# The second product of an MLP by seven half-size products instead of eight, tokens in chunks of 256

## The chip, the core and the metric

The kernel runs on one core of a Trainium2 chip. The core has a tensor engine (PE, with its weight loads shown apart as PEld), VectorE (DVE), ScalarE (ACT), GpSimd (POOL) and a queue that issues transfers (SP). The metric is the device time of one execution in microseconds, as the median of several runs. A profile shows one execution, instruction by instruction.

## The reference

Clustered attention makes `x` of shape (4, 768, 512): four batches, eight heads, each query attends to the keys of its own cluster. What follows is a token mix of rank 32 and an MLP with a residual:

```python
h = xt @ U @ V                      # xt = x with tokens last
u = x + h.transpose(0, 2, 1)        # (4, 768, 512)
ch = np.maximum(u @ w_ch1, 0.0) @ w_ch2   # 512 -> 2048 -> 512
return (u + ch).astype(np.float32)
```

The weights reach the kernel as the bits of float64 numbers, and the kernel turns them into float32 itself.

## The kernel before

**Order of work.** Everything is written as a plan: `at(time, fn, *args)` enters a call with a due time in plan units, the list is sorted by time, and the calls are issued in that order. `keep_order` ties the instructions of each engine to that order, so an engine never overtakes its own queue. Attention takes 16 head pairs of 12 units; the MLP begins at `M0`, in plan units, and there one unit was one inner tile of one chunk. The last of attention and of the mix (`values`, `sums`, `normalise`, `mix_u`, `mix_sum`, `mix_v`) is due after M0 and is interleaved with the first units of the MLP.

**Split products.** A float32 matrix is held as a high part, rounded to the type fp32r, and a low part, the remainder. A product is the sum of three: high x high, high x low, low x high. So each logical matmul is three instructions, each with a weight load of 128 columns.

**The MLP.** The 3072 tokens were eight chunks of 384 (`nh = 2 * B`), the 2048 inner features 16 tiles `f` of 128. For each chunk `turn_u` transposes the rows `u` (L595) and writes the parts `uh` and `ul` (ACT L597, DVE L598). `gemm1(i, f)` is 4 x 3 matmuls of 384 columns into a PSUM tile `ps_h` (L606 to L608); then ACT writes `hh`, the high part of relu (L611), and DVE `hl`, the low part (L612). `gemm2(i, f)` comes 1.2 units later: for each of three token tiles three matmuls of 512 columns (L622 to L624), accumulated over all 16 tiles in a bank `y`. `finish(i)` adds `y` to `u` on DVE (L630) and sends it out (L631).

**The weights.** Four groups `g` of four inner tiles. `load_weights(g, step, stage)` takes one raw tile [128, 512] through six stages with the due times in `stages`: a DMA into `rw` (L151), `upper` on ACT (L159) into `rw_g`, three bit operations on DVE, `join` (L171 to L174 in one go for groups 0 and 1; L178, L180, L183 for groups 2 and 3) into `rw_t`, and last the split: the high part on ACT (L204), the low part on POOL, or for a few tiles of group 1 on DVE (L205). Group 0 is made early in attention, group 1 in its last five head pairs' time, groups 2 and 3 while the MLP runs. Group 1 and 2 lie in `arena`, the space of attention's operands.

**Near M0.** `weights` (L492) adds up the attention weights `T`, mostly on POOL, for some steps of the last pair on DVE. All PSUM tiles of attention, transposes and `gemm1` are turned round in one pool of four, `ps_w`; `y` has four banks of its own.

Of the kernel before, what the change touches and what calls it, by code (L numbers as in the profile page):

```python
# [117 lines left out]
def clustered_attention_moe(ctx: ExitStack, tc: tile.TileContext, qk, v, cen, moe_U, moe_V, w1, w2, out):  # L118
# [8 lines left out]
    raw = ctx.enter_context(tc.tile_pool(name="raw", bufs=2))  # L127
    rows = ctx.enter_context(tc.tile_pool(name="rows", bufs=2, side="right"))
    ps_w = ctx.enter_context(tc.tile_pool(name="ps_w", bufs=4, space=PSUM, side="right"))

# [23 lines left out]
    def upper(rw):  # L154

        r, n = rw.shape
        g = raw.tile([P, 512], F32, name="rw_g")[0:r, 0:n]
        high = rw.bitcast(I32).rearrange("p (n two) -> p n two", two=2)[:, :, 1].bitcast(F32)
        nc.scalar.mul(g, high, 2.0 ** -112)  # L159
        return rw, g.bitcast(I32), None  # L160

    def join(rw, g, t, k):
# [4 lines left out]
        if k is None:  # L167

            b = work("ps_t").bitcast(I32)[0:r, 0:n]
            t = raw.tile([P, 512], I32, name="rw_t")[0:r, 0:n]  # L170
            nc.vector.tensor_scalar(b, g, 3, None, op0=ALU.logical_shift_left)  # L171
            nc.vector.scalar_tensor_tensor(out=b, in0=g, scalar=-0x80000000, in1=b,
                                           op0=ALU.bitwise_and, op1=ALU.bitwise_or)
            nc.vector.scalar_tensor_tensor(out=t, in0=low, scalar=29, in1=b,  # L174
                                           op0=ALU.logical_shift_right, op1=ALU.bitwise_or)
        elif k == 0:
            t = raw.tile([P, 512], I32, name="rw_t")[0:r, 0:n]
            nc.vector.tensor_scalar(t, g, 3, None, op0=ALU.logical_shift_left)  # L178
        elif k == 1:
            nc.vector.scalar_tensor_tensor(out=t, in0=g, scalar=-0x80000000, in1=t,  # L180
                                           op0=ALU.bitwise_and, op1=ALU.bitwise_or)
        else:
            nc.vector.scalar_tensor_tensor(out=t, in0=low, scalar=29, in1=t,  # L183
                                           op0=ALU.logical_shift_right, op1=ALU.bitwise_or)
        return rw, g, t

    parts, pool = {}, {}

    def load_weights(g, step, stage):
# [4 lines left out]
        elif stage == 1:  # L194
            parts[g, step] = upper(parts[g, step])
        elif stage < 5:
            if g > 1:
                parts[g, step] = join(*parts[g, step], stage - 2)
            elif stage == 3:
                parts[g, step] = join(*parts[g, step], None)  # L200
        else:
            w = parts.pop((g, step))[2].bitcast(F32)
            hi, lo = wg[g][2 * k][:, i, :], wg[g][2 * k + 1][:, i, :]
            nc.scalar.copy(hi, w)  # L204
            (nc.vector if g == 1 and step in (1, 2, 3, 5) else nc.gpsimd).tensor_sub(lo, w, hi)  # L205


    def weight_tile(g, name, pool):
        return pool.tile([P, 4, 512], F32R, name=f"{name}{g}", bufs=1)

    names = ("w1h", "w1l", "w2h", "w2l")
# [11 lines left out]

    wg[1] = [in_arena(2 * XS + 2048 * k, 4, 512) for k in range(4)]
    wg[2] = [in_arena(2048 * k, 4, 512) for k in range(3)]

# [36 lines left out]

    c_sb = raw.tile([P, 512], F32, name="rw_g").rearrange("p (n d) -> p n d", n=NP)
    c_rn = one.tile([P, NP], F32, name="c_rn")
    c_sq = raw.tile([P, 512], F32, name="rw_g")[:, 0:NP * D].rearrange("p (n d) -> p n d", n=NP)
    c_n = [one.tile([P, NP], F32, name=f"c_n{k}") for k in range(3)]
# [37 lines left out]
    def load_mix(k, stage):  # L305
# [17 lines left out]

# [24 lines left out]
    def largest(i):  # L348
# [218 lines left out]

    nh = 2 * B

    free = 2 * XS + 4 * 2048  # L570
    turned = {0: [in_arena(free, ND, HS), in_arena(free + ND * HS, ND, HS)]}

    def open_mlp():
# [3 lines left out]
        pool["y"] = ctx.enter_context(tc.tile_pool(name="ps_y", bufs=4, space=PSUM, reuse_waits="tile"))  # L577
        wg[2].append(weight_tile(2, "w2l", sb))
        turned[1] = [sb.tile([P, ND, HS], F32R, name=name) for name in ("uh", "ul")]

    def open_weights():
        tail.close()
        right = ctx.enter_context(tc.tile_pool(name="wpool3", bufs=1, side="right", reuse_waits="tile"))
        wg[3] = [weight_tile(3, name, right) for name in names]

    def fetch_u(i):
        b, h = divmod(i, 2)
        live["u", i] = rows.tile([P, HT, DM], F32, name="u", tag="R")
        nc.sync.dma_start(out=live["u", i], in_=u_scr[b][:, h * HT:(h + 1) * HT, :])

    def turn_u(i, d):

        ps = work("ps_uT")
        for t in range(HT):
            nc.tensor.transpose(ps[:, t * P:(t + 1) * P], live["u", i][:, t, d * P:(d + 1) * P], ident)  # L595
        hi, lo = (x[:, d, :] for x in turned[i % 2])
        nc.scalar.copy(hi, ps[:, 0:HS])  # L597
        nc.vector.tensor_sub(lo, ps[:, 0:HS], hi)  # L598

    def gemm1(i, f):  # L600
        w1h, w1l, _, _ = wg[f // FG]
        uh, ul = turned[i % 2]
        fs = slice((f % FG) * P, (f % FG) * P + P)
        ps = work("ps_h")
        for d in range(ND):
            nc.tensor.matmul(ps[:, 0:HS], w1h[:, d, fs], uh[:, d, :], start=(d == 0), stop=False)  # L606
            nc.tensor.matmul(ps[:, 0:HS], w1h[:, d, fs], ul[:, d, :], start=False, stop=False)  # L607
            nc.tensor.matmul(ps[:, 0:HS], w1l[:, d, fs], uh[:, d, :], start=False, stop=(d == ND - 1))  # L608
        hh = pool["sb"].tile([P, HS], F32R, name="hh", bufs=3)
        hl = pool["sb"].tile([P, HS], F32R, name="hl", bufs=3)  # L610
        nc.scalar.activation(hh, ps[:, 0:HS], AF.Relu)  # L611
        nc.vector.scalar_tensor_tensor(out=hl, in0=ps[:, 0:HS], scalar=0.0, in1=hh, op0=ALU.max, op1=ALU.subtract)  # L612
        live["h", i, f] = hh, hl

    def gemm2(i, f):
        if f == 0:
            live["y", i] = [pool["y"].tile([P, 512], F32, name=f"y_{t}", tag="y") for t in range(HT)]
        y, (hh, hl) = live["y", i], live.pop(("h", i, f))
        _, _, w2h, w2l = wg[f // FG]
        for t in range(HT):  # L620
            ts = slice(t * P, (t + 1) * P)
            nc.tensor.matmul(y[t], hh[:, ts], w2h[:, f % FG, :], start=(f == 0), stop=False)  # L622
            nc.tensor.matmul(y[t], hh[:, ts], w2l[:, f % FG, :], start=False, stop=False)  # L623
            nc.tensor.matmul(y[t], hl[:, ts], w2h[:, f % FG, :], start=False, stop=(f == NF - 1))  # L624

    def finish(i):
        b, h = divmod(i, 2)
        u, y = live.pop(("u", i)), live.pop(("y", i))
        for t in range(HT):
            nc.vector.tensor_add(u[:, t, :], y[t], u[:, t, :])  # L630
            nc.sync.dma_start(out=out[b, (h * HT + t) * P:(h * HT + t + 1) * P, :], in_=u[:, t, :])  # L631

# [83 lines left out]
    for g, pace in enumerate((NS, 2.04, 1, 1)):  # L716
        for stage, step in enumerate(stages[f"g{g}"]):
# [4 lines left out]
    at(M0 + 8.05, open_weights)  # L722
    for i in range(nh):
        m = M0 + NF * i
        at(m + (-10.98 if i else -15.06), fetch_u, i)
        for d in range(ND):
            at(m + (-4.5 + d if i else -1.52), turn_u, i, d)
        for f in range(NF):
            at(m + f, gemm1, i, f)
            at(m + f + 1.2, gemm2, i, f)  # L730
        at(m + 16.35, finish, i)

# [32 lines left out]
```

## Time and profile before

| | us |
|---|---|
| median of 3 runs | 1021.26 (1020.79 to 1023.74) |
| span of the profiled execution, first to last instruction | 1018.5 |
| PE busy | 990.5 |
| PEld busy | 786.9 |
| DVE busy | 490.5 |
| ACT busy | 347.7 |
| POOL busy | 359.4 |
| first `gemm1` matmul starts at | 463.13 |
| last matmul starts at | 1014.21 |

The median of the runs lies 2.8 us above the span. Busy time of PE is not PE at its peak: matmuls are pipelined and their shown durations overlap, so the distance from one start to the next tells what a matmul costs in a stream. A line such as `L606` is the line of the kernel above; `y<-w2l,hh` reads as output and inputs; `x288` is a count. In a list of groups the last columns are busy time, mean ns of one, the idle time of that engine before them and what ended it.

### The profile page before, as it was taken

Reading aid. Unit: us, or ns where it says so; the run is one execution under the profiler, and the core shown is the slowest. Engines: PE = TensorE matmul, PEld = TensorE weight load, DVE = VectorE, ACT = ScalarE, POOL = GpSimd, SP = SyncE. Lnnn points to the kernel's source line nnn. Section 1 sums busy time; section 2 is a strip of 40 time slices with the busy share of each in tenths; the row PEclk is TensorE's granted clock in tenths of the full one; section 3 lists DMA queues with packets and bytes.
Section 4 is the critical chain, followed back from the end, with each engine's and each line's share of the span. In section 5 each row is a group of like instructions: output and inputs, shape, how many; then the busy total and the mean of one; then the engine's idle time right before and its main releaser. Section 6 shows DMA issues by size and latency. Waiting matters only on the chain.

```text
span 1018.5 us, 13723 instructions
## 1 busy us (share of the span) xinstructions
PE 990.5 (97%) x5368; PEld 786.9 (77%) x5368; DVE 490.5 (48%) x914; ACT 347.7 (34%) x572; POOL 359.4 (35%) x246
## 2 busy tenths in 40 slices
PE   5899999999999999989999999999999999999998
PEld 3566666676667666657899999999999999998997
DVE  5797777777777666768772121121221211212211
ACT  4454554555556554564341111111111111111110
POOL 5466676888788967753230000000000000000000
PEclk9899999999999999999999999999999999999999
DMA  7754554656465636243431001010010010100000
GB/s 186 191 130 115 157 146 122 192 155 156 100 199 136 150 86 181 61 143 108 163 123 63 1 32 32 1 62 1 1 63 1 18 46 1 62 1 1 32 1 32
DMA packets 28687, 87.71 MB, mean 86 GB/s; under 512 B 4880, under 2 KB 9488, under 8 KB 28112
## 3 DMA queue, kind: packets, MB, share of 16 engines
q1 hardware_dynamic: 28240, 86.76, 30.5%
q8 instruction: 42, 0.69, 0.3%
q14 instruction: 21, 0.17, 0.1%
q10 hardware_dynamic: 384, 0.10, 0.0%
HBM read 42.99 MB, written 12.58 MB: 55 GB/s over the span
## 4 chain that ended last, share of the span: by engine, by line
PE 90%; DVE 5%; ACT 1%; issue 1%; POOL 1%; DMA 1%; ACTq 0%; SPq 0%; POOLq 0%; DVEq 0%
PE o_ps L500 12%; PE ps_h L606 9%; PE ps_h L608 9%; PE ps_h L607 9%; PE y L624 9%; PE y L623 9%; PE y L622 9%; PE ps_max L453 7%; PE st L477 6%; PE st L479 6%; DVE m L455 2%; PE ps_sum L512 1%; PE ps_sim L343 1%; PE ps_oT L533 1%; PE ps_uT L595 1%
## 5 line engine op out<-in xcount | busy, mean ns | idle before, releaser
L492 POOL TENSOR_TENSOR T<-T,pr 128x768 f32<-128x768 f32 x120 | 226.5, 1887 | 44.9 <-ACT pr L482 19.3
L612 DVE SCALAR_TENSOR_TENSOR hl<-ps_h,hh 128x384 fp32r<-128x384 f32 x128 | 71.2, 556 | 349.9 <-ACT hh L611 349.8
L455 DVE TENSOR_REDUCE m<-ps_max 128x1 f32<-128x384 f32 x384 | 195.2, 547 | 80.6 <-PE ps_max L453 79.0
L611 ACT ACTIVATE hh<-ps_h 128x384 fp32r<-128x384 f32 x128 | 62.9, 491 | 373.8 <-PE ps_h L608 373.8
L482 ACT ACTIVATE pr<-st 128x768 f32<-128x768 f32 x192 | 154.3, 812 | 83.5 <-PE st L479 65.4
L453 PE MATMUL ps_max<-arena 128*128 128x384 f32 x384 | 126.6, 380 | 6.9 <-DVE oh L369 2.5
L500 PE MATMUL o_ps<-pr,vt 128*64 128x384 f32 x768 | 132.2, 494 | 0.1
L623 PE MATMUL y<-w2l,hh 128*128 128x512 f32 x288 | 113.6, 395 | 0.0
L477 PE MATMUL st<-arena 128*128 128x384 f32 x384 | 104.9, 354 | 2.0 <-ACT pr L482 2.0
L453 PEld LDWEIGHTS ps_max<-arena 128*128 128x128 f32 x384 | 70.5, 192 | 45.4 <-issue 21.4
L500 PEld LDWEIGHTS o_ps<-pr,vt 128*64 128x64 f32 x768 | 52.7, 138 | 66.4 <-issue 59.8
L479 PE MATMUL st<-arena 97*128 97x384 f32 x384 | 99.2, 340 | 2.8 <-DMA arena<-mT 2.8
L477 PEld LDWEIGHTS st<-arena 128*128 128x128 f32 x384 | 66.2, 190 | 17.9 <-issue 9.3
L492 POOL TENSOR_TENSOR T<-pr 128x768 f32<-128x768 f32 x30 | 56.6, 1886 | 62.2 <-ACT pr L482 62.2
L624 PE MATMUL y<-w2h,hl 128*128 128x512 f32 x192 | 76.1, 396 | 0.0
L624 PE MATMUL y<-arena,hl 128*128 128x512 f32 x192 | 76.0, 396 | 0.0
L622 PE MATMUL y<-w2h,hh 128*128 128x512 f32 x192 | 75.1, 391 | 0.0
L622 PE MATMUL y<-arena,hh 128*128 128x512 f32 x192 | 74.8, 390 | 0.0
L479 PEld LDWEIGHTS st<-arena 97*128 97x128 f32 x384 | 70.4, 190 | 3.5 <-issue 2.2
L623 PEld LDWEIGHTS y<-w2l,hh 128*128 128x128 f32 x288 | 54.0, 188 | 9.1
L504 ACT COPY os<-o_ps 128x384 f32<-128x384 f32 x32 | 15.3, 480 | 104.7 <-PE o_ps L500 104.7
L606 PE MATMUL ps_h<-arena,w1h 128*128 128x384 f32 x128 | 44.8, 350 | 0.2 <-DVE arena L598 0.2
(132 smaller groups left out, 1597.3 us busy)
## 6 DMA issues: line engine op xcount, KB each, us to landing
rw<-in_w SPq DMA_DIRECT2D x32, 512.0 KB
R<-in_qk SPq DMA_DIRECT2D x32, 384.0 KB
arena<-arena SPq DMA_DIRECT2D x32, 384.0 KB
arena<-arena SPq DMA_DIRECT2D x64, 192.0 KB
vt<-in_v SPq DMA_DIRECT2D x16, 384.0 KB
u_scr<-xt SPq DMA_DIRECT2D x4, 1536.0 KB
u<-u_scr SPq DMA_DIRECT2D x8, 768.0 KB
out_y<-u SPq DMA_DIRECT2D x24, 256.0 KB
```

The costliest lines, as they stand in the source:

```text
L453: nc.tensor.matmul(ps[:, 0:HS], x1[:, 0, g // 2, g % 2, t * P:(t + 1) * P], x1[:, 1, h, g % 2, :], start=True, stop=True)
L455: nc.vector.reduce_max(live["m2", i][:, h, u:u + 1], ps[:, 0:HS], axis=AX.X)
L477: nc.tensor.matmul(st[:, j, 0:HS], x1[:, 1, hk, j, ks], x1[:, 0, h, j, :], start=True, stop=False)
L479: nc.tensor.matmul(st[:, j, 0:HS], x2[0:97, 1, hk, j, ks], x2[0:97, 0, h, j, :], start=False, stop=True)
L482: nc.scalar.activation(pr, st[:, :, 0:HS], AF.Exp, scale=SCALE)
L492: eng.tensor_add(T, live["p", i, h, 0] if c == 1 else T, live["p", i, h, c])
L500: nc.tensor.matmul(o_ps[64 * j:64 * j + 64, 0:HS], vv[:, c, j, :], pr[:, j, :], start=(c == 0), stop=(c == NT - 1))
L606: nc.tensor.matmul(ps[:, 0:HS], w1h[:, d, fs], uh[:, d, :], start=(d == 0), stop=False)
L607: nc.tensor.matmul(ps[:, 0:HS], w1h[:, d, fs], ul[:, d, :], start=False, stop=False)
L622: nc.tensor.matmul(y[t], hh[:, ts], w2h[:, f % FG, :], start=(f == 0), stop=False)
L623: nc.tensor.matmul(y[t], hh[:, ts], w2l[:, f % FG, :], start=False, stop=False)
L624: nc.tensor.matmul(y[t], hl[:, ts], w2h[:, f % FG, :], start=False, stop=(f == NF - 1))
```

## The change

The second product, for the inner tiles 4 to 15, is made with Strassen's method in its Winograd form. A pair `p` of two inner tiles, two token tiles and two halves of 256 output columns make a 2 x 2 block product; it takes seven products of half size in place of eight. Each is still three matmuls (high and low parts), now of 256 columns. Tiles 0 to 3 (pairs 0 and 1) are computed as before. It brings with it:

- Tokens go in 12 chunks of 256 (two token tiles); the first product's matmuls have 256 columns, and one PSUM tile holds the two inner tiles of a pair.
- For a Strassen pair, `gemm1` writes relu in float32 into `xs` (ACT), makes four more sums of it on DVE, and `halves` makes the high parts `xh` (ACT, 7 x 128 columns) and the low parts `xl` (DVE, the same). `xl` has one buffer, `xs` one, `xh` two.
- For w2 of groups 1 to 3, `load_weights` makes four sums of two raw tiles on DVE into PSUM, and splits the seven blocks: four with the low part on DVE, three on POOL.
- `gemm2` accumulates the seven products in four `y` banks over a session; `finish` puts them together with ten DVE operations and an ACT copy.
- The first two chunks are each cut into two sessions (chunk 0 pairs 0 to 3, chunk 1 pairs 0 to 5, chunk 0 pairs 4 to 7, chunk 1 pairs 6 and 7); the other chunks are one session each.
- A plain pair takes 1.34 plan units, a Strassen pair 1.25. The stages of group 3 move later, and its pace goes from 1 to 0.9. `rw_g` and `mx` have one buffer instead of two, and the mix weights lose a copy.

```diff
-    "g1":   (-26.11, -21.73, -21.19,  -20.5,  -20.5, -18.29),
-    "g2":   ( -2.37,  -1.48,  -0.87,  -0.52,  -0.75,   0.36),
-    "g3":   (  5.26,   6.37,   6.46,   6.74,   7.45,   8.06),
+    "g1":   (-26.11, -21.73, -21.19,  -20.5,  -20.5,  -18.6),
+    "g2":   ( -2.37,  -1.48,  -0.87,  -0.52,  -0.75,    0.1),
+    "g3":   (   7.2,    8.3,    8.6,   8.75,    8.9,    9.2),
...
+    def halve(hi, lo, w, eng):
+        nc.scalar.copy(hi, w)
+        eng.tensor_sub(lo, w, hi)
...
+        elif not (k and g):
+            w = parts.pop((g, step, "t")).bitcast(F32)
+            halve(wg[g][2 * k][:, i, :], wg[g][2 * k + 1][:, i, :], w,
+                  nc.vector if g == 1 and step in (1, 2, 3, 5) else nc.gpsimd)
+        elif i % 2:
...
+            a, b = (work(name).rearrange("p (s n) -> p s n", s=2) for name in ("ps_a", "ps_b"))
+            less(a[:, 0], t1[:, 1], t1[:, 0])
+            less(a[:, 1], t1[:, 1], t2[:, 1])
+            less(b[:, 0], t2[:, 1], a[:, 0])
+            less(b[:, 1], t2[:, 0], b[:, 0])
+            halve(hi[:, 3:5], lo[:, 3:5], a, nc.vector)
+            halve(hi[:, 5:7], lo[:, 5:7], b, nc.vector)
+            halve(hi[:, 0], lo[:, 0], t1[:, 0], nc.gpsimd)
+            halve(hi[:, 1:3], lo[:, 1:3], t2, nc.gpsimd)
...
+        for j in range(2):
+            fs = slice((2 * p + j) % FG * P, (2 * p + j) % FG * P + P)
+            to = ps[:, 2 * P * j:2 * P * j + 2 * P]
+            for d in range(ND):
+                nc.tensor.matmul(to, w1h[:, d, fs], uh[:, d, :], start=(d == 0), stop=False)
+                nc.tensor.matmul(to, w1h[:, d, fs], ul[:, d, :], start=False, stop=False)
+                nc.tensor.matmul(to, w1l[:, d, fs], uh[:, d, :], start=False, stop=(d == ND - 1))
+        live["ps", c, p] = ps
+        if p > 1:
+            xs = live["xs", c, p] = live.pop("xs") if "xs" in live else pool["sb"].tile([P, 8, P], F32, name="xs")
+            nc.scalar.activation(xs[:, 0:4].rearrange("p s n -> p (s n)"), live.pop(("ps", c, p)), AF.Relu)
+            nc.vector.tensor_sub(xs[:, 4], xs[:, 0], xs[:, 1])
+            nc.vector.tensor_tensor(out=xs[:, 5:7], in0=xs[:, 0:8:4],
+                                    in1=xs[:, 2].unsqueeze(1).broadcast_to([P, 2, P]), op=ALU.add)
+            nc.vector.tensor_sub(xs[:, 7], xs[:, 3], xs[:, 6])
...
+            xs = live.pop(("xs", c, p))
+            nc.scalar.copy(xh, xs[:, 1:8])
+            nc.vector.tensor_sub(xl, xs[:, 1:8], xh)
+
+    sessions = [(0, 0, 4), (1, 0, 6), (0, 4, 8), (1, 6, 8)] + [(c, 0, 8) for c in range(2, NC)]
+
+    products = ((0, 0, 2, 0), (2, 1, 0, 0), (6, 2, 0, 1), (1, 6, 1, 0), (4, 3, 3, 0), (5, 5, 2, 1), (3, 4, 3, 1))
...
+            wh, wl = wg[p // 2][2][p % 2]
+            for pairs in (((xl, wh),), ((xh, wh), (xh, wl))):
+                for a, b, bank, half in products:
+                    for x, w in pairs:
+                        add(bank, y[bank][:, 256 * half:256 * half + 256], x[:, a], w[:, b],
+                            p == last - 1 and w is wl and (half == 1 or bank == 1))
...
+        add(u1, y[0], u1)
...
+        nc.scalar.copy(s0, y[2][:, m2])
+        add(s1, y[2][:, m3], s0)
+        add(u1[:, m2], u1[:, m2], s0)
+        add(s0, y[3][:, m3], s1)
+        add(u2[:, m2], u2[:, m2], s0)
+        add(s1, y[3][:, m2], s1)
+        add(u1[:, m3], u1[:, m3], s1)
+        add(s0, y[3][:, m2], s0)
+        add(u2[:, m3], u2[:, m3], s0)
...
+    for _, _, p in units:
+        begin.append(m)
+        m += 1.34 if p < 2 else 1.25
...
+        at(begin[k], gemm1, c, p)
+        at(begin[k] + 0.72, halves, c, p)
+        at(begin[k + 1] + 0.7, gemm2, s, c, p)
+        if p == sessions[s][2] - 1:
+            at(begin[k + 1] + 0.75, finish, s)
```

More of the change, by code (lines that the diff above doesn't have):

```diff
@@ L169, in join @@
             b = work("ps_t").bitcast(I32)[0:r, 0:n]
[L170 removed]
+            t = b if t is None else t
             nc.vector.tensor_scalar(b, g, 3, None, op0=ALU.logical_shift_left)
@@ L600, in gemm1 @@
[L600 to L603, printed above, removed]
-        ps = work("ps_h")
[L605 to L631, printed above, removed]
+        wg[3] = [weight_tile(3, name, right) for name in ("w1h", "w1l")]
+        wg[3].append([[seven_tile(3, f"{name}_{k}", right) for name in ("w2h", "w2l")] for k in range(2)])
+    def fetch_u(c):
+        b, r = divmod(c, 3)
+        if c > 1 and c % 2 == 0:
+            live["u", c] = raw.tile([P, 512], I64, name="rw").bitcast(F32).rearrange("p (t d) -> p t d", t=2)
+            live["s", c] = raw.tile([P, 512], F32, name="rw_g", bufs=1).rearrange("p (t d) -> p t d", t=2)
+        else:
+            u = rows.tile([P, 6, 256], F32, name="u", tag="R")
+            live["u", c] = u[:, 0:4].rearrange("p (t k) d -> p t (k d)", t=2)
+            live["s", c] = u[:, 4:6]
+        nc.sync.dma_start(out=live["u", c], in_=u_scr[b][:, 2 * r:2 * r + 2, :])
@@ new lines, in turn_u, with gemm1 @@
+    def turn_u(c, d0):
+        ps = work("ps_uT")
+        for d in range(d0, d0 + 2):
+            for slot, t in enumerate((1, 0)):
+                to = (2 * (d - d0) + slot) * P
+                nc.tensor.transpose(ps[:, to:to + P], live["u", c][:, t, d * P:(d + 1) * P], ident)
+        hi, lo = (x[:, d0:d0 + 2, :].rearrange("p d n -> p (d n)") for x in turned[c % 2])
+        nc.scalar.copy(hi, ps)
+        nc.vector.tensor_sub(lo, ps, hi)
+    def gemm1(c, p):
+        w1h, w1l, _ = wg[p // 2] if p > 1 else (*wg[0][0:2], None)
+        uh, ul = turned[c % 2]
+        ps = work("ps_h")
+        for j in range(2):
[13 more added lines that the diff above has]
+            nc.vector.tensor_sub(xs[:, 7], xs[:, 3], xs[:, 6])
@@ new lines, in clustered_attention_moe, with gemm2, add @@
+    sessions = [(0, 0, 4), (1, 0, 6), (0, 4, 8), (1, 6, 8)] + [(c, 0, 8) for c in range(2, NC)]
+    products = ((0, 0, 2, 0), (2, 1, 0, 0), (6, 2, 0, 1), (1, 6, 1, 0), (4, 3, 3, 0), (5, 5, 2, 1), (3, 4, 3, 1))
+    def gemm2(s, c, p):
+        first, last = sessions[s][1:]
+        if p == first:
+            live["y", s] = [pool["y"].tile([P, 512], F32, name=f"y_{t}", tag="y") for t in range(4)]
+            live["begun"] = set()
+        y, begun, (xh, xl) = live["y", s], live["begun"], live.pop(("h", c, p))
+        def add(bank, to, lhs, rhs, stop=False):
+            nc.tensor.matmul(to, lhs, rhs, start=bank not in begun, stop=stop)
+            begun.add(bank)
+        if p < 2:
+            _, _, w2h, w2l = wg[0]
+            for x, w in ((xl, w2h), (xh, w2h), (xh, w2l)):
+                for j in range(2):
+                    for t in range(2):
+                        add(t, y[t], x[:, 2 * j + 1 - t], w[:, 2 * p + j, :])
+        else:
+            wh, wl = wg[p // 2][2][p % 2]
[4 more added lines that the diff above has]
+                            p == last - 1 and w is wl and (half == 1 or bank == 1))
@@ new lines, in finish @@
+    def finish(s):
+        c, first, last = sessions[s]
+        b, r = divmod(c, 3)
+        u, y = live["u", c], live.pop(("y", s))
+        u1, u2 = u[:, 0], u[:, 1]
+        s0, s1 = (live["s", c][:, k] for k in range(2))
+        add = nc.vector.tensor_add
+        m2, m3 = (slice(0, 256), slice(256, 512))
+        add(u1, y[0], u1)
+        if first < 2:
+            add(u2, y[1], u2)
+        else:
+            add(u2[:, m2], y[1][:, m2], u2[:, m2])
+        nc.scalar.copy(s0, y[2][:, m2])
[7 more added lines that the diff above has]
+        add(u2[:, m3], u2[:, m3], s0)
+        if last == NPR:
+            for t in range(2):
+                nc.sync.dma_start(out=out[b, (2 * r + t) * P:(2 * r + t + 1) * P, :], in_=u[:, t])
```

107 lines of the change are left out of this document (58 added, 49 removed).

## The prediction

> **What bounds the kernel now.** I read the page first (span, busy row, chain of waits), then busy time by stretches, then the timeline at a few places.
>
> ```profile
> span 1018.5 us, 13723 instructions
> PE 990.5 (97%) x5368; PEld 786.9 (77%) x5368; DVE 490.5 (48%) x914; ACT 347.7 (34%) x572; POOL 359.4 (35%) x246
> ...
> PE 90%; DVE 5%; ACT 1%; issue 1%; POOL 1%; DMA 1%; ACTq 0%; SPq 0%; POOLq 0%; DVEq 0%
> ```
>
> The tensor engine is busy 97% of the span and holds 90% of the chain. The share of VectorE, 48%, is a mean over unlike stages, so I take the MLP apart: the tail of attention with the weights of groups 2 and 3 still coming in (463 to 535.7), and a later chunk without them.
>
> ```profile
> 463.00:472.00 9.00, 8.87 (x52) 7.55 (x53) 7.68 (x14) 4.77 (x10) 3.56 (x3) 1.00 0.40 111
> 472.00:505.00 33.00, 33.00 (x167) 27.58 (x166) 27.32 (x41) 12.88 (x23) 9.69 (x8) 1.00 0.40 124
> 505.00:535.70 30.70, 30.70 (x162) 27.66 (x161) 19.98 (x30) 12.03 (x24) 10.02 (x8) 1.00 0.45 152
> 603.97:672.25 68.28, 68.28 (x349) 61.72 (x348) 12.94 (x23) 9.79 (x20) 0.00 (x0) 1.00 0.07 24
> ```
>
> The columns are the stretch, its length, busy time of PE, weight loads, DVE, ACT, POOL, then granted clock and DMA. PE never rests and its clock is 1.00. In the steady chunk DVE works 12.94 of 68.28 us. In the first chunk, 72.7 us, it works 7.68 + 27.32 + 19.98 = 55.0 us; between 472 and 505 it is 83% busy. So the MLP is bound by PE throughout, with DVE close behind at its start. What a matmul costs there:
>
> ```profile
> 571.27 0.39 PE L622 MATMUL y<-arena,hh 128*128 128x512 f32 x1
> ...
> 573.35 0.33 PE L606 MATMUL ps_h<-uh,arena 128*128 128x384 f32 x1
> ...
> 575.46 0.39 PE L622 MATMUL y<-arena,hh 128*128 128x512 f32 x1
> ```
>
> Nine products of 512 columns take 573.35 - 571.27 = 2.08 us, 0.231 each; twelve of 384 take 2.11 us, 0.176 each. What counts is start to start; the durations shown overlap.
>
> **The change, part by part.** *Columns on PE.* A chunk of 256 tokens now has 8 pairs x 24 = 192 first-product matmuls of 256 columns, 24 second-product matmuls of 512 for the plain pairs, 6 x 21 = 126 of 256 for the Strassen pairs, and 8 transposes. The columns of the second product fall from 24 halves to 21 on three quarters of the tiles; the number of matmuls with their weight loads rises from 336 per 384 tokens to 342 per 256. No fp32r matmul of 256 columns is in the trace, so I bound it. By columns it is 0.231/2 = 0.116 us; along the line through both sizes, 0.176 - (0.231 - 0.176) = 0.121 us. A floor is the weight load:
>
> ```profile
> 586.13 0.19 PEld L606 LDWEIGHTS ps_h<-uh,w1h 128*128 128x128 f32 x1
> ...
> 586.24 0.19 PEld L607 LDWEIGHTS ps_h<-ul,w1h 128*128 128x128 f32 x1
> 517.80 0.33 PE ps_uT L595 x3
> ```
>
> Behind the short transposes a load follows the one before after 0.11 us, though each is shown at 0.19, and three transposes take 0.33 us. So loads allow 0.110, and 256 columns lie just above that floor. I take 0.119, between the two estimates. A chunk is then 318 x 0.119 + 24 x 0.231 + 8 x 0.11 = 44.3 us, twelve are 531 us; before, 8 x 68.28 = 546 us. **PE term: -15 us**, and each ns on the short matmul is 318 x 12 = 3816 ns. At 0.116 the term is -26, at 0.121 it is -7, at the load floor -49, at 0.125 it is +8.
>
> The Trainium skill, "TensorE: Matmul & The Clock Gate", section "Back-to-back issue gap", gives N/2.4 + 2.5 ns for one matmul, an estimate of 109 ns at 256 columns by that page. For 384 and 512 columns it gives 162 and 216 ns where the rows above show 176 and 231: the trace does not agree, and what would follow is a rival below.
>
> *Work on DVE at the start of the MLP.* This is the part that I think decides. The rows that price it:
>
> ```profile
> L183 DVE SCALAR_TENSOR_TENSOR rw_t<-rw,rw_t 128x512 int32<-128x512 int32 x16 | 20.5, 1284 | 0.3
> L180 DVE SCALAR_TENSOR_TENSOR rw_t<-rw_g,rw_t 128x512 int32<-128x512 int32 x16 | 11.8, 745 | 0.3
> L612 DVE SCALAR_TENSOR_TENSOR hl<-ps_h,hh 128x384 fp32r<-128x384 f32 x16 | 8.8, 551 | 6.1 <-ACT hh L611 5.9
> L178 DVE TENSOR_SCALAR rw_t<-rw_g 128x512 int32<-128x512 int32 x16 | 7.8, 490 | 8.8 <-ACT rw_g L159 8.8
> ...
> L598 DVE TENSOR_TENSOR ul<-ps_uT,uh 128x384 fp32r<-128x384 f32 x4 | 2.2, 548 | 0.0
> L598 DVE TENSOR_TENSOR arena<-ps_uT,arena 128x384 fp32r<-128x384 f32 x4 | 1.9, 550 | 0.0
> 444.94 0.95 DVE L492 TENSOR_TENSOR T<-pr 128x768 f32<-128x768 f32 x1
> 452.32 0.69 DVE L205 TENSOR_TENSOR arena<-rw_t,arena 128x512 fp32r<-128x512 f32 x1
> 496.86 1.87 DVE L563 TENSOR_TENSOR xt<-ps_h,xt 128x512 f32<-128x512 f32 x3
> ```
>
> 512 columns take 0.69 us and 768 take 0.95, about 1 ns a column and 0.17 fixed: 128 columns 0.30, 256 0.43, 896 1.08. A Strassen pair then costs DVE two times 0.30, one 0.43 and one 1.08, 2.1 us; a plain pair 0.69; a drain of the four y banks 0.69 + 9 x 0.43 = 4.6 us; the sums of one pair of w2 tiles 4 x 0.43 + 2 x 0.69 = 3.1 us. Until the weights of group 3 are in use (two sessions, then pairs 4 to 6 of chunk 0) there are 4 plain and 9 Strassen pairs, 2 drains, 4 pairs of weight tiles and 4 turns of 0.69: 2.8 + 18.9 + 9.2 + 12.4 + 2.8 = 46 us, some 41 us when the overlap of neighbours is taken off, one tenth by the last row (3 x 0.69 in 1.87). Out of the 55.0 us go L612 and L598, 8.8 + 2.2 + 1.9 = 13 us. DVE has 42 + 41 = 83 us to do. PE has 4 x (24 x 0.119 + 12 x 0.231) + 9 x 45 x 0.119 = 71 us, and 72.6 - 68.3 = 4 of attention and 2 of transposes, 77 us in all. So DVE, which was the idler one, becomes the longer one. At 100% it would be 6 us late; at the 83% of its densest stretch, where each wait on ACT or DMA also costs it time, 83/0.83 = 100, 23 us late. Little of it can hide: gemm2 of a pair waits for the xl that DVE writes last, behind 24 + 21 matmuls (5.4 us) of cover, of which the chain of that pair alone (ACT's relu, three sums, ACT's copy, xl) uses 0.6 + 1.0 + 0.9 + 1.1 = 3.6 by these rows:
>
> ```profile
> L482 ACT ACTIVATE pr<-st 128x768 f32<-128x768 f32 x192 | 154.3, 812 | 83.5 <-PE st L479 65.4
> ...
> L611 ACT ACTIVATE hh<-ps_h 128x384 fp32r<-128x384 f32 x128 | 62.9, 491 | 373.8 <-PE ps_h L608 373.8
> ```
>
> A drain, or the join of one raw tile (L178, L180 and L183, 2.5 us) queued ahead of xl, is then already too long. Weights themselves are not late: group 3 is needed 15.4 units after M0, before at 12. **DVE term: +18 us**, nearer to the measured 83% than to a full engine; ends 0 and +25.
>
> One more thing works against DVE:
>
> ```profile
> 510.46 1.32 DVE L183 SCALAR_TENSOR_TENSOR rw_t<-rw,rw_t 128x512 int32<-128x512 int32 x1
> 509.78 1.44 POOL L205 TENSOR_TENSOR w1l<-rw_t,w1h 128x512 fp32r<-128x512 f32 x1 [4.23 <-ACT w1h L204]
> ```
>
> L183 takes 1.32 us when it meets a POOL subtraction, and ends 0.56 after it; undisturbed, 512 columns take 0.69. The Trainium skill, "SBUF — State Buffer", section "Who interferes with whom", says that a DVE instruction with two SBUF inputs and a GpSimd one that reads SBUF exclude each other; these rows agree. The sums, xl and half of each drain are of that kind, so the term is rather low than high.
>
> *Before the MLP.* The sums for the w2 of group 1 land in the last 20 us of attention, 3.1 us each in place of one L205, the second between the T additions:
>
> ```profile
> 458.20 2.02 DVE T L492
> ...
> 461.66 0.95 DVE T L492
> 462.61 0.48 DVE arena L598
> 463.13 0.44 PE ps_h L606
> ```
>
> These rows of the chain of waits run from DVE's additions straight to the first gemm1. The second 3.1 us go into that queue with PE waiting behind it: **+3.5 us** with some of the first (ends 0 and 6). The single rw_g and mx buffers cost nothing there: each is read out before the next is written by the plan's own order.
>
> *Drains and sessions.* A session takes all four y banks, yet the next gemm2 begins 24 matmuls later, 2.9 us, and from the fifth session on with plain pairs, which need only the first two banks, free after 0.69 + 0.43. I cost that at 0; without that cover it would be up to 3 us for each of 13 sessions.
>
> *The end.*
>
> ```profile
> 1013.25 2.09 DVE L630 TENSOR_TENSOR u<-y,u 128x512 f32<-128x512 f32 x3 [1.73 <-PE y L624]
> ...
> 1013.97 1.73 SPq L631 DMA_DIRECT2D out_y<-u  x3
> ...
> 1014.21 0.40 PE L624 MATMUL y<-w2h,hl 128*128 128x512 f32 x1
> ```
>
> Now only one addition follows the last matmul; then about seven dependent ones of 0.43 do, 3.0 us for 0.7: **+2 us** (ends 1 and 4).
>
> *Sum:* -15 + 18 + 3.5 + 2 = +8.5 us on a span of 1018.5, 1027. The runs' median lies 2.8 us above that span, which I add for what lies around it: **1030 us**.
>
> **The rivals.** (1) *DVE keeps up and the columns count.* PE term -26 (0.116), DVE 6, M0 2, end 2: -16, so 1005 us. For it: the 83% holds waits that more work would fill, and between the last join of group 2 and the first of group 3 lie two units without any. Against: 83 us of work against 77. The sign turns where DVE is less than 9 us late at 0.119. (2) *Gain and lateness cancel*, DVE about 10 late: 1021 us. (3) *The short matmul costs more than its columns*, because each carries a load as long as itself: at 0.125 the PE term is +8, and with 14 + 3.5 + 2 the time is 1049 us. It decides from 0.123 on, where the PE term is nil. For it: 0.176 is already above what 384/512 of 0.231 gives (0.173), so something is fixed per matmul. Against: 0.11 between loads. (4) *Only the load floor counts*, 0.109: 38 us more on PE, DVE later by 3: 995 us. That is where the page's gap formula leads too.
>
> **How the numbers follow.** Forecast 0.42 (its own range 1022 to 1040); rival 1 0.27, rival 2 0.13, rival 3 0.13, rival 4 0.05. The range 1003 to 1047 leaves out rival 4 and the far part of rival 3. About 0.3%, 3 us, is what a measurement can tell from none: faster 0.32 (rivals 1 and 4), within 0.3% 0.13, slower 0.55 (forecast and rival 3).
>
> **What would show it.** In chunks 3 to 12 each gemm1 block of 24 should last 2.86 us and a chunk 44.3; a block of 2.78 or less speaks for rivals 1 and 4, 3.0 for rival 3. In the first 90 us of the MLP, PE should have gaps before gemm2 released by DVE's xl, 18 us in sum, with DVE over 85% busy; without gaps the DVE term is wrong. The first gemm1 should start near 466.5, and the last matmul should lie 6 us before the end. Forecast and sign fall if DVE's sums run beside ACT's waits and PE does not notice.

## The result, and the profile after

The changed kernel takes 1056.12 us (median of 4 runs, 1053.59 to 1059.35); the kernel before, run beside it, 1021.76 us (4 runs, 1020.79 to 1023.74). The ratio is 1.0339, 95% interval 1.0316 to 1.0363: slower, as forecast, but by 34 us where 8.5 were forecast, and outside the range.

The page of the changed kernel, the lines that answer to those of before (forty slices of the span in the rows of digits):

```profile
span 1053.7 us, 17112 instructions
PE 993.8 (94%) x6784; PEld 823.5 (78%) x6784; DVE 641.2 (61%) x1240; ACT 419.5 (40%) x630; POOL 354.8 (34%) x247
PE   5899999999999999789697899999999999999996
DVE  5786677777777766687868644444453444534444
PEclk8898999999999999899898999999999999999999
PE 44%; DVE 4%; issue 2%; ACT 2%; DVEq 0%; ACTq 0%
```

PE fell from 97% to 94% of the span and DVE rose from 48% to 61%. The dents in PE's row, from the 17th digit to the 23rd, lie between about 420 and 600 us: the end of attention and the first two chunks of the MLP. The clock row has its dents in the same place and three at the very beginning. From about 600 us on, both are full.

The two spans differ by 1053.7 - 1018.5 = 35.2 us. Three starts on PE cut that difference into parts.

| | before | after | difference |
|---|---|---|---|
| start to first `gemm1` | 463.13 | 474.50 | +11.4 |
| first `gemm1` to start of the last matmul | 551.1 | 572.3 | +21.2 |
| start of the last matmul to the end | 4.3 | 6.9 | +2.6 |

The middle part holds a gain and a loss. Busy time by stretches, with the columns as before (stretch, length, busy PE, weight loads, DVE, ACT, POOL, granted clock, DMA):

```profile
474.50:600.04 125.54, 104.35 (x716) 94.12 (x717) 96.36 (x170) 45.84 (x79) 20.67 (x17) 0.92 0.26 80
500.68:540.88 40.20, 30.37 (x171) 26.04 (x172) 29.29 (x56) 11.96 (x22) 4.50 (x5) 0.83 0.26 86
644.37:688.79 44.42, 44.42 (x352) 43.44 (x351) 19.49 (x38) 12.00 (x18) 0.00 (x0) 1.00 0.07 24
```

A steady chunk takes 44.42 us, and twelve of them 533.0, against 8 x 68.28 = 546.2 before: 13.2 us gained. The first two chunks, which share their time, take 125.5 us instead of 2 x 44.42 = 88.8. With the 4.9 us of attention and mix that the middle part held before too (551.1 - 546.2), the loss there is 125.5 - 88.8 - 4.9 = 31.8; PE is idle for 125.54 - 104.35 = 21.2 us of it. The 31.8 is an estimate, good to some 2 us: the stretch ends before the second product of its last pair (it holds 279 of the 300 second-product matmuls of two chunks, and 21 x 0.119 = 2.5 us), and the 4.9 leaves out the first chunk's 12 transposes, which lie ahead of the middle part (12 x 0.11 = 1.3). The remaining 2.6 of 21.2 + 13.2 = 34.4 lie in the ten chunks behind, over their 44.42; most of it is that second product.

The clock is the second thing to see: 0.92 in the first row, 0.83 in the densest 40 us, where before it was 1.00. And DVE, 96.36 of 125.54, is busy 77% of the time, not over 85%.

What PE waited for there, from the timeline (start, duration, what ran, and in brackets the idle time ahead of it and what ended it):

```profile
506.16 1.09 PE L688 MATMUL y<-arena,xl 128*128 128x256 f32 x7 [1.49 <-DVE xl L673]
512.66 1.65 PE L585 MATMUL ps_h<-x,v 96*128 96x512 f32 x3 [3.73 <-DVE x L579]
526.20 1.39 PE L585 MATMUL ps_h<-x,v 96*128 96x512 f32 x2 [2.72 <-DVE w2l L191]
```

and from the list of waits between 474 and 601 us (line that waited, line waited for: sum, times, longest), one row of ACT and the five longest of PE:

```profile
ACT rw_g L160 <- DVE rw_t L180: 18.3, 7, 3.5
PE y L688 <- DVE xl L673: 7.4, 5, 3.2
PE ps_h L585 <- DVE x L579: 3.7, 1, 3.7
PE y L688 <- DVE u L725: 3.5, 2, 2.1
PE ps_h L585 <- DVE w2l L191: 2.7, 1, 2.7
PE ps_h L645 <- DVE xl L669: 1.5, 2, 1.0
```

The five rows of PE make 18.8 of its 21.2 us. Every releaser is DVE, but only the second row, 7.4 us, is the one foretold. The last two need reading, for there PE waits for a PSUM tile: `mix_v` (L585) takes one of the four tiles of `ps_w`, and with the sums of w2 lying in two tiles of the same pool (`ps_a`, `ps_b`) it got none until DVE had split them (L191); a first product (L645) got none until DVE had read a plain pair's (L669). The row with L725 is a session that waits until the drain of an earlier one has read its `y` bank. The first row is no wait of PE: ACT stands before its next raw tile because the one `rw_g` is still being read by DVE's bit operations, and `xs`, `xh` and the high parts of w2 are queued behind it on ACT.

The same wait appears long before the MLP, in ACT's timeline:

```profile
68.78 0.55 ACT L160 ACTIVATE rw_g<-rw 96x384 f32<-96x384 f32 x1 [3.04 <-DVE ps_t L173]
85.53 0.55 ACT L160 ACTIVATE rw_g<-rw 96x384 f32<-96x384 f32 x1 [1.86 <-DVE ps_t L173]
```

The plan has the mix tile k+1's `upper` due at 14.22 and the join of tile k at 15.04: with one buffer the first must wait for the second, and the softmax work behind it waits too. The score matmuls of attention, each set against the same one of the kernel before, are 0.5 us later at about 82 us (times of the kernel before), 6.2 at 114, 6.0 still at 430, and 10.3 to 10.6 at 452.

### The profile page after: what moved, and what is told of

Its sections match the earlier page's. It is cut to its first block, busy times and chain, and to the rows that moved or that the text cites. A ratio compares the mean times of both kernels' runs of the same rounds, so it can differ in the third digit from the quotient of the medians.

```text
span 1053.7 us, 17112 instructions
## 1 busy us (share of the span) xinstructions
PE 993.8 (94%) x6784; PEld 823.5 (78%) x6784; DVE 641.2 (61%) x1240; ACT 419.5 (40%) x630; POOL 354.8 (34%) x247
## 4 chain that ended last, share of the span: by engine, by line
PE 44%; DVE 4%; issue 2%; ACT 2%; DVEq 0%; ACTq 0%
PE y L688 20%; PE ps_h L647 8%; PE ps_h L645 8%; PE ps_h L646 8%; PE ps_uT L631 1%; DVE xl L673 1%; ACT xh L672 0%; DVE rw_t L180 0%; ACT w2h L190 0%; DVE rw_t L178 0%; ACT xs L651 0%; DVE xs L653 0%; DVE rw_t L183 0%; ACT rw_g L160 0%; DVE xs L652 0%
## 5 line engine op out<-in xcount | busy, mean ns | idle before, releaser
L673 DVE TENSOR_TENSOR xl<-xs,xh 128x896 fp32r<-128x896 f32 x72 | 79.5, 1104 | 73.0 <-ACT xh L672 73.0
L651 ACT ACTIVATE xs<-ps_h 128x512 f32<-128x512 f32 x72 | 43.1, 599 | 195.9 <-PE ps_h L647 190.7
L652 DVE TENSOR_TENSOR xs<-xs 128x128 f32<-128x128 f32 x72 | 21.3, 296 | 160.3 <-ACT xs L651 160.3
L645 PE MATMUL ps_h<-uh,w1h 128*128 128x256 f32 x384 | 110.8, 289 | 1.4 <-DVE xl L669 1.0
L688 PE MATMUL y<-w2l,xh 128*128 128x256 f32 (+1 forms) x432 | 110.7, 310 | 0.0
L645 PE MATMUL ps_h<-uh,arena 128*128 128x256 f32 x384 | 109.4, 285 | 0.4 <-DVE xl L669 0.4
L647 PE MATMUL ps_h<-uh,arena 128*128 128x256 f32 x384 | 109.4, 285 | 0.0
L647 PE MATMUL ps_h<-uh,w1l 128*128 128x256 f32 x384 | 108.8, 283 | 0.0
L672 ACT CAST xh<-xs 128x896 fp32r<-128x896 f32 x72 | 67.9, 943 | 81.8 <-DVE xs L655 81.7
L688 PE MATMUL y<-w2h,xh 128*128 128x256 f32 (+1 forms) x348 | 89.2, 316 | 0.0
L688 PEld LDWEIGHTS y<-w2l,xh 128*128 128x128 f32 x432 | 83.9, 194 | 3.9
```

What stands on the lines that cost most here:

```text
L645: nc.tensor.matmul(to, w1h[:, d, fs], uh[:, d, :], start=(d == 0), stop=False)
L647: nc.tensor.matmul(to, w1l[:, d, fs], uh[:, d, :], start=False, stop=(d == ND - 1))
L673: nc.vector.tensor_sub(xl, xs[:, 1:8], xh)
L688: nc.tensor.matmul(to, lhs, rhs, start=bank not in begun, stop=stop)
```

## The experiments

**How the runs are read.** d is the length of the first two chunks of the MLP, 125.5 us in the changed kernel. M is the start of the first `gemm1`, 474.5. Both come from a single profiled execution. The rest, from the end of d to the start of the last matmul, is 446.8 us in every kernel run here but one (447.2 with `xl` on POOL), so the times differ by what comes before it. Two theories are tried: that single buffers and places in a queue make others wait (`rw_g`, the `y` banks), and that DVE simply has too much to do in d. The first two experiments are on the former: does the one `rw_g` cost what the prediction put at nothing?

**Two buffers for the mix tiles alone.** The raw tiles of the mix go through `rw_t`, which has two.

```diff
-    def upper(rw):
+    def upper(rw, name="rw_g", bufs=1):
...
-        g = raw.tile([P, 512], F32, name="rw_g", bufs=1)[0:r, 0:n]
+        g = raw.tile([P, 512], F32, name=name, bufs=bufs)[0:r, 0:n]
...
-            parts["mix", k] = upper(parts["mix", k])
+            parts["mix", k] = upper(parts["mix", k], "rw_t", 2)
```

> The raw tiles of the mix go into rw_t (two buffers) instead of the single rw_g; nothing else differs from the changed kernel. Theory A (a single rw_g makes ACT's next bit scaling wait for DVE, with the exponentials of attention queued behind it): the 3.0 and 1.9 us waits of ACT between 65 and 86 us go, every scores matmul from 110 us on starts 6 us earlier, and the time falls by 6 us to about 1050. Rival (those waits were cover for something else that comes late anyway, such as DVE's own joins): less than 2 us, 1055 or so.

1054.04 us, ratio 1.0311 (1.0296 to 1.0327). ACT's waits for DVE at `rw_g` between 60 and 120 us are gone and the lateness at 114 us falls from 6.2 to 2.2 us. At 430 us it is 3.1 against 6.0, at 452 us 8.2 against 10.3, and only 2 us are left in the time, where the theory wanted 6; the two intervals overlap. So the wait cost 4 us where it occurred, and about half of that was lost again later.

**No `rw_g` at all.** ACT scales the high words where they lie in `rw`, and the bit operations read them there. So no raw tile, of the mix or the MLP, waits for that buffer.

```diff
-        r, n = rw.shape
-        g = raw.tile([P, 512], F32, name="rw_g", bufs=1)[0:r, 0:n]
-        high = rw.bitcast(I32).rearrange("p (n two) -> p n two", two=2)[:, :, 1].bitcast(F32)
-        nc.scalar.mul(g, high, 2.0 ** -112)
-        return rw, g.bitcast(I32), None
+        high = rw.bitcast(I32).rearrange("p (n two) -> p n two", two=2)[:, :, 1]
+        nc.scalar.mul(high.bitcast(F32), high.bitcast(F32), 2.0 ** -112)
+        return rw, high, None
```

> ACT scales the high words inside rw itself, so no raw tile needs rw_g and none waits for one; the bit operations on DVE read them at a stride. Theory A (the single rw_g holds ACT, and behind it exp, relu, xs and xh): the 6 us of the early stage, 3 of the 4.5 us lost between 425 and 475 us and some 5 to 10 of the 32 us of the first two chunks go: 1037 to 1043. Theory B (DVE simply has too much work at the start of the MLP): only the early 6 us and perhaps 2 of the second come back, and the strided reads on DVE add up to 4 us: 1048 to 1052.

1046.55 us, ratio 1.0234 (1.0214 to 1.0253): 9.6 us less than the changed kernel, between the two forecasts; the profiled executions differ by 7.1 (1053.7 and 1046.6). M is 469.9, 4.6 earlier.

```profile
469.90:592.90 123.00, 103.83 (x716) 94.11 (x717) 95.94 (x170) 45.88 (x79) 20.36 (x17) 0.93 0.26 82
```

d shrinks by 2.5 only, and with it PE's idle time to 19.2. The single buffer was thus a cost of its own, mostly ahead of the MLP; the 30 us inside the first two chunks have another cause. The experiments that follow start from this kernel, all but the next one.

**`xl` on POOL.** In the changed kernel, the low parts `xl` of the first two chunks go to POOL, which is nearly free there.

```diff
-            nc.vector.tensor_sub(xl, xs[:, 1:8], xh)
+            (nc.gpsimd if c < 2 else nc.vector).tensor_sub(xl, xs[:, 1:8], xh)
```

> In the first two chunks POOL instead of DVE writes xl: 10 subtractions of 1.1 us go from DVE, and POOL, busy under 20% there, takes about 2.3 us for each. Theory B (DVE's work): 8 to 11 us less, 1045 to 1048. Rival (the chain of one pair, relu to xl, is what PE waits for): 1.2 us longer for each pair and more behind POOL's own subtractions, 5 to 12 us more, 1061 to 1068.

1059.91 us, ratio 1.0367 (1.0351 to 1.0382): 4 us slower still by the medians, though the two intervals overlap; d is 3.4 longer. Theory B's gain of 8 to 11 us is absent. DVE is relieved of 11 operations in d, and PE waits for `xl` longer than the 7.4 us above:

```profile
475.70:604.60 128.90, 105.61 (x717) 95.91 (x718) 93.02 (x159) 45.57 (x79) 47.01 (x28) 0.91 0.25 78
```

```profile
PE y L688 <- POOL xl L673: 13.5, 7, 5.9
```

One `xl` takes a median of 2.5 us on POOL against the 1.10 us on DVE in the group row below, and it is the last link of a pair's chain. DVE's busy time fell by 3.3 us only, where 11 operations of 1.10 would be 12: its other operations took longer (the 16 of L183 17.4 us in place of 11.1). This says nothing yet against too much work on DVE; it says that the length of the chain to `xl` counts as well.

```profile
L673 DVE TENSOR_TENSOR xl<-xs,xh 128x896 fp32r<-128x896 f32 x72 | 79.5, 1104 | 73.0 <-ACT xh L672 73.0
```

**Three kinds of DVE work, left out one at a time.** Each run is the kernel without `rw_g`, with one kind of work left out.

(a) The joins of groups 2 and 3 do only the first of their three bit operations; the sign and low bits of these weights are left out.

```diff
-            if g > 1 or stage == 3:
+            if stage == (2 if g > 1 else 3):
```

> As inplace, and for the weights of groups 2 and 3 only the first of the three bit operations on DVE is made (sign and low bits are left out): 32 operations of 0.7 us, 22 us of DVE, go between 475 and 570 us. Theory B (DVE's work): nearly all that is left of the idle time and of the halved clock in the first two chunks goes, 18 to 28 us below inplace, to 1015 to 1025. Rival (the chain relu, xs, xh, xl of a pair, or the waits for raw tiles, is too long in itself): less than 8 us below inplace.

(b) The w2 sums and their low parts on DVE are left out; ACT copies raw tiles to their places.

```diff
-            less(a[:, 0], t1[:, 1], t1[:, 0])
...
-            halve(hi[:, 5:7], lo[:, 5:7], b, nc.vector)
+            for part in (hi, lo):
+                nc.scalar.copy(part[:, 3:5], t1)
+                nc.scalar.copy(part[:, 5:7], t2)
```

> As inplace, but the four sums of each pair of w2 tiles, and the two low parts of them that DVE makes, are left out; ACT copies the raw tiles into those places instead (4 copies of 0.6 us for 2). DVE loses 3.1 us for each of 6 pairs, and ps_a and ps_b no longer take two of the four PSUM buffers. Theory B (DVE's work, and the PSUM tiles that wait for it): the first gemm1 3 us earlier, the first two chunks 8 to 12 us shorter, 1032 to 1037. Rival (the chain of a pair, the drains or the halved clock after a few long waits set the stage): under 5 us in all, 1042 or more.

(c) The drains of the first two sessions stop after the additions of the first two banks.

```diff
+        if s < 2:
+            return
         nc.scalar.copy(s0, y[2][:, m2])
```

> As inplace, but the drains of the first two sessions make only their two first additions; eight DVE operations and an ACT copy of each are left out, and y banks 2 and 3 are free at once. My theory: the 2 us waits for y at the start of each of sessions 3 and 4 go (they begin with Strassen pairs and need all four banks), DVE loses 3.4 us twice: 6 to 10 us, 1037 to 1041. The prediction's step (drains cost nothing beside their DVE time): 3 to 4 us, 1043.

The first two chunks of the three runs, in this order:

```profile
468.40:582.20 113.80, 100.85 (x716) 92.84 (x717) 72.15 (x138) 45.54 (x79) 20.23 (x17) 0.94 0.28 89
```

```profile
468.90:583.40 114.50, 100.70 (x716) 92.36 (x717) 83.73 (x146) 49.98 (x87) 19.81 (x17) 0.94 0.27 88
```

```profile
466.90:579.40 112.50, 100.03 (x716) 91.22 (x717) 89.92 (x154) 45.28 (x77) 20.75 (x17) 0.95 0.28 90
```

| left out | time, us | ratio | d, us | DVE busy in d |
|---|---|---|---|---|
| nothing | 1046.55 | 1.0234 (1.0214 to 1.0253) | 123.0 | 95.9 |
| (a) two thirds of the joins | 1038.00 | 1.0154 (1.0137 to 1.0171) | 113.8 | 72.2 |
| (b) w2 sums | 1038.34 | 1.0162 (1.0147 to 1.0177) | 114.5 | 83.7 |
| (c) two drains | 1035.74 | 1.0143 (1.0120 to 1.0167) | 112.5 | 89.9 |

(a) missed its forecast: 24 us of DVE work taken out bring 9.2 us of d and 8.5 us of time, where the theory that DVE's sum of work decides wanted more than twice that. (b) fell short by a little. (c) beat its forecast: 6 us of DVE work bring 10.5. A microsecond of DVE work is thus worth 0.4 us of d in the joins, 0.7 in the sums (12.2 us for 8.5), and 1.7 in the drains. What an operation costs seems to depend on what it stands in front of: a drain stands in front of `xl` and holds the `y` banks besides. This is argued, not shown, since (b) also gives back two PSUM tiles of `ps_w` and (c) two `y` banks, and neither was tried without the other.

**All three left out together.** The edits (a), (b) and (c) in one kernel.

> All three cuts together: two of three bit operations, the sums of w2 with their low parts, and the two early drains. Theory B: DVE has 47 us less to do in all, the first two chunks take 94 to 98 us (their products, transposes and the rest of attention), the granted clock stays at 1.00 there, 1014 to 1020. Rival (something else holds PE there: raw tiles from DMA, ACT's order, the chain of a pair): 105 us or more, over 1026.

1021.63 us (10 runs), ratio 1.0003 (0.9993 to 1.0014).

```profile
470.40:567.30 96.90, 93.51 (x717) 87.33 (x718) 54.55 (x98) 49.35 (x85) 19.43 (x17) 1.00 0.31 104
```

d is 96.9, inside its forecast; the time just misses its own, because attention was late in this kernel too (M at 470.4). The cuts add up to 9.2 + 8.5 + 10.5 = 28.2 alone and bring 26.1 together: nearly additive. Set this row beside the one of the kernel without `rw_g`, with 716 and 717 matmuls in the stretch. Of the 26.1 us, PE's idle time gives 19.2 - 3.4 = 15.8, and PE's busy time gives 103.83 - 93.51 = 10.3, at a clock of 0.93 against 1.00. So the DVE work, with the tiles and banks that it holds, costs about 16 us as waits and about 10 us as slower matmuls, for the same matmuls.

**Does the clock cost by itself?** In the records of the changed kernel the granted clock falls to 0.50 during PE's waits or soon after them and stays there for 3.4 or 6.8 us. For this test 16 matmuls of 512 columns, whose result is overwritten, go ahead of the first `mix_v` matmul of the last batch, where PE had its 3.73 us wait in the changed kernel. The wait cannot get shorter by it, but PE is not idle in it.

```diff
         ps = work("ps_h")
+        for _ in range(16 if (b, t) == (B - 1, 0) else 0):
+            nc.tensor.matmul(ps, v3[:, 0:P], wg[0][0][0:96, 0, :], start=True, stop=True)
```

> As inplace, with 16 matmuls of 512 columns more, into the PSUM tile of the first mix_v of the last batch, which the real matmul then overwrites. They fill the 3.7 us in which PE waits for x3 at about 503 us. Theory C (a long wait costs twice: the wait itself, and the halved clock that follows it): the half-clock stretch that begins about 5 us after that wait goes or shrinks, and the first two chunks are 1.5 to 4 us shorter although PE does 3.7 us more work. Rival (the clock is a bystander, DVE's lateness sets the pace): the same length within 1 us, since PE then meets the next wait earlier.

1045.61 us, ratio 1.0234 (1.0213 to 1.0255). The kernel without `rw_g`, then this one, in the 8 us around the place (each is shifted by M):

```profile
508.00:516.00 8.00, 7.74 (x37) 6.62 (x37) 7.76 (x17) 0.00 (x0) 0.00 (x0) 0.80 0.21 67
```

```profile
506.00:514.00 8.00, 6.20 (x37) 5.06 (x37) 7.76 (x17) 0.00 (x0) 0.00 (x0) 1.00 0.22 67
```

The clock there is 1.00 instead of 0.80 and the same 37 matmuls are busy 1.5 us less, but d is only 1.0 shorter (122.0), as the rival had it, and the next halved stretch, 6.8 us from 514.8, stays. DVE is busy for 7.76 of 8 us in both: while DVE is late, a faster PE arrives earlier at the next wait. So the 10 us of slower matmuls are real as busy time, but it isn't shown that they would be won without the waits going too.

**The joins later.** The weights of the second half of group 2 come 2.5 plan units later and those of group 3 come 1.6 later, to spread DVE's work.

```diff
-                at(step + pace * k + (M0 if g else 0), load_weights, g, k, stage)
+                later = 1.6 if g == 3 else 2.5 if g == 2 and k > 3 else 0
+                at(step + pace * k + later + (M0 if g else 0), load_weights, g, k, stage)
```

> As inplace, with the w2 tiles of group 2 taken 2.5 plan units later and all of group 3 1.6 units later; the same work on DVE, less of it at the drain of session 1 and the end of the mix. Theory D (DVE's bursts set the stalls, more than its total): 5 to 12 us less in the first two chunks, 1035 to 1041. Theory B (the amount of DVE's work): within 3 us of inplace, since it is only late elsewhere, or worse if weights of group 3 come late.

1045.76 us, ratio 1.0231 (1.0216 to 1.0247).

```profile
470.80:591.00 120.20, 100.62 (x717) 91.78 (x718) 95.75 (x170) 46.48 (x79) 19.96 (x17) 0.96 0.26 84
```

d is 2.8 shorter, and the time the same within its scatter. Moving work within the first two chunks is worth little while the work stays.

**The mix tiles as before the change.** The change had also shortened the way of the mix weights: the bit operations end in PSUM and the copy is left out. Here they go through `rw_t` again, with their last stage two later.

```diff
-            rw, high, _ = parts.pop(("mix", k))
+            rw, high, _ = parts["mix", k]
+            r, c = rw.shape
+            parts["mix", k] = join(rw, high, raw.tile([P, 512], I32, name="rw_t")[0:r, 0:c], None)
+        elif stage == 5:
+            w = parts.pop(("mix", k)).bitcast(F32)
             if k:
-                w = join(rw, high, None, None).bitcast(F32)
```

> As inplace, with the mix weights taken as before the change (through rw_t, with a cast of their own at the last stage) instead of through a PSUM tile that is held for the casts. Theory: of the 2 to 4 us by which attention is still behind the kernel before at 110 us, 2 or more come back. Rival: it is the single mx or the clock's own phase, and the lateness at 110 us stays within 1 us.

1042.01 us, ratio 1.0202 (1.0185 to 1.0219), by the medians another 4.5 us less than without `rw_g` alone; the two intervals overlap slightly. M is 464.6, 1.5 us from the kernel before; the lateness at 114 us is 0.0, and the clock isn't halved in attention after its start.

```profile
464.60:586.30 121.70, 103.02 (x717) 93.59 (x718) 95.93 (x170) 45.85 (x79) 20.31 (x17) 0.93 0.25 83
```

d hardly moves. The two edits of the raw tiles bring M from 474.5 to 469.9 and 464.6: that is 9.9 of the 11.4 us that attention had lost. M scatters between kernels that are nearly alike up to there (466.9 to 470.8 in the seven without `rw_g`, 464.6 to 467.0 in the three with the old mix), so the share of each edit is good to some 2 us.

**The two last combinations.** First the old mix with all three cuts (work left out as in a, b and c):

> inplace_oldmix with the three cuts of inplace_bare: attention as fast as before the change, and DVE relieved of 47 us at the start of the MLP by leaving two of three bit operations, the sums of w2 with their low parts, and the two early drains out. Theory: the first gemm1 near 464.6, the first two chunks 97, the other ten 446.8 us as in every kernel so far: 1015 to 1017, 5 to 6 us under the kernel before; what is left of the gain on PE then stands free. Rival (PE's gain is not there, and the time of inplace_bare only came near the kernel before by its cuts elsewhere): 1020 or more.

1019.37 us (11 runs), ratio 0.9977 (0.9969 to 0.9986), between the two expectations. d is 96.9, as with the other mix:

```profile
467.00:563.90 96.90, 93.47 (x716) 87.29 (x717) 54.64 (x98) 49.44 (x85) 19.47 (x17) 1.00 0.31 104
```

Second, the old mix with the joins later, the complete computation:

> inplace_oldmix with the later weights of inplace_later; it computes everything. If the two gains add (4.5 and 3 us): 1038 to 1040, still slower than the kernel before, since DVE has the same work to do. Rival: they overlap, 1041 to 1043.

1042.31 us, ratio 1.0210 (1.0195 to 1.0226): no better than the old mix alone, and d is 120.7 with four halved stretches in it. The gains overlap. Of the kernels that compute everything the best one stays 2% behind the kernel before, and none beats it.

## Why the prediction was right in sign and wrong in size

**Columns on PE: right.** Starts of three consecutive matmuls in a steady chunk, from the timeline:

```profile
644.37 0.28 PE L645 MATMUL ps_h<-uh,w1h 128*128 128x256 f32 x1
644.49 0.28 PE L646 MATMUL ps_h<-ul,w1h 128*128 128x256 f32 x1
644.61 0.28 PE L647 MATMUL ps_h<-uh,w1l 128*128 128x256 f32 x1
```

0.12 us from start to start, median 0.119 to 0.120, where 0.119 was taken. A chunk came out at 44.42 (44.3 forecast), the term at -13.2 (-15). Rivals 3 and 4, a short matmul of 0.125 or of 0.109, are refuted. The Trainium skill, "TensorE: Matmul & The Clock Gate", section "Back-to-back issue gap", has a formula for the isolated matmul that gives the latter as an estimate; the trace does not agree with it here.

**DVE in the first chunks: right cause, mis-sized.** It was +18; idle time is 21.2, and the loss of that stretch is 31.8. Three things in the step failed. It put the loss down to gaps before `gemm2` that `xl` ends, 18 us in sum; these are 7.4 us, and 9.9 are waits for x3, for a drain and for the w2 sums (3.7, 3.5 and 2.7). It set DVE's 83 us against PE's 77 and took DVE to be the longer engine, over 85% busy; DVE was 77% busy, and the three cuts were worth 0.4, 0.7 and 1.7 us for one of work. The loss comes in single waits, behind stretches in which DVE is full (7.76 of 8 us in the rows above), and not from an engine that is full throughout; what share each place in the queue has stays open. And the step priced only idle time: the matmuls behind the waits ran at half the clock, 10.3 us of busy time more than in the kernel with all three cuts. The cuts together show how much hung on DVE: 26.1 of d.

**Before the MLP: +3.5 against +11.4, and the wrong reason.** The step that failed reads "The single rw_g and mx buffers cost nothing there: each is read out before the next is written by the plan's own order". The plan's order is the reverse for the mix tiles. Without `rw_g` and with the old way of the mix tiles, M is 464.6 to 467.0 where 463.1 was that of before, so the two hold 7.5 to 9.9 of the 11.4. The reason that the prediction gave, the sums for the w2 of group 1, is not borne out: without them M is 468.9 against 469.9, within the scatter. The single `mx` was not tried by itself.

**Drains and sessions: 0 was wrong.** "A session takes all four y banks, yet the next gemm2 begins 24 matmuls later" holds in a steady chunk. In the first two, DVE comes to the drain late: two waits for `y` of 3.5 us in sum, and 10.5 us of d when two drains are cut to their first two additions. That the four tiles of `ps_w` must also hold the w2 sums was not in the prediction at all; it is the wait of 2.72 us at `mix_v`.

**The end: +2 against +2.6, right.**

```profile
1046.19 0.69 DVE L713 TENSOR_TENSOR u<-y,u 128x512 f32<-128x512 f32 x1 [1.91 <-PE y L688]
...
1050.29 0.42 DVE L726 TENSOR_TENSOR u<-u 128x256 f32<-128x256 f32 x1
```

The last matmul starts at 1046.84 and DVE's last addition ends at 1050.71; the transfer and the end of the program follow.

**What stays open.** How the 10 us of slower matmuls would come back by themselves: one halved stretch taken away brought 1.0 us. And why M stays 1.5 to 3.9 us late with the old mix: halved stretches at 89.5 and 454.7 us stand in the old mix with all three cuts, and none in the old mix alone, though the two kernels differ little up to there.

**What the method could win here.** The gain is 13.2 us of columns less 2.6 at the end, about 10.6 us or 1%. With the old mix and the three cuts, the middle part is 96.9 + 446.8 = 543.7 against 551.1, so 7.4 of the 13.2 arrive; M is 3.9 late and the end 2.6 longer. That leaves 7.4 - 3.9 - 2.6 = 0.9 us, which is the difference of the two profiled spans (1018.5 and 1017.6); the ratio of 0.9977 makes it 2.4.

## What to carry to other kernels

Before trading an engine that is 97% busy for work on another one, look at the stretch where the other is busiest, and list for each new operation what stands behind it on its queue: the price of a microsecond was 0.4 to 1.7 us here, with the PSUM tiles and banks that the work held. Where a change takes a buffer away to make room, read the due times of its next writer and its last reader; if the writer is due first, its whole engine waits. And do not price a wait of PE by its length alone: here some 16 us of waits came with some 10 us of slower matmuls, though one halved stretch taken away by itself brought only 1.0 us.

## What the runs showed of the hardware that was not expected

**The clock is halved after short waits.** Three windows of the changed kernel in which part or all of the time has a halved clock:

```profile
80.00:90.00 10.00, 8.13 (x43) 5.74 (x39) 8.61 (x17) 5.50 (x9) 3.85 (x3) 0.91 0.18 53
90.00:100.00 10.00, 9.91 (x47) 6.01 (x51) 4.03 (x9) 2.34 (x4) 7.00 (x4) 0.74 0.68 157
440.00:445.00 5.00, 2.90 (x8) 1.54 (x10) 3.49 (x4) 2.81 (x5) 4.76 (x4) 0.50 0.31 103
```

Between 90 and 100 us PE is busy for 9.91 of 10 us with only 47 matmuls. The halved stretches of the changed kernel are at 88.3, 115.6, 439.9, 511.5, 525.2, 566.2 and 576.4 us, each 3.4 or 6.8 us long; the kernel before has one, at 435.9, apart from its start and end. The Trainium skill, "TensorE: Matmul & The Clock Gate", section "Part 1: The HAM clock gate (the "warmup" mystery)", says that the clock goes to 4/8 after an idle window of about 3.4 us and back after a busy one. The granted 0.50 and the lengths agree; the idle window doesn't, for in none of these seven had PE been idle for 3.4 us when the clock fell. The same page of the Trainium skill, section "Why this matters for your kernels", puts the limit at gaps above about 3 us; here the stretch at 525.2 came with a wait of 2.72 us, from 523.5 to 526.2, and ahead of the one at 115.6 the only waits in 20 us were these two, of 0.95 and 0.83 us:

```profile
113.52 0.44 PE L476 MATMUL ps_max<-arena 128*128 128x384 f32 x1 [0.95 <-DVE v L343]
114.79 0.28 PE L488 MATMUL ps_mT<-ident,m 128*12 128x128 f32 x1 [0.83 <-DVE m L483]
```

**A subtraction of 896 columns took 2.5 us on POOL and 1.10 us on DVE**, so POOL's idle time is not a place for the last link of a chain.
